# Attention and a gated convolution block on one Trainium2 core: the diagonal masks of the first seven pairs as 64-row blocks, and a start planned with the port shared by DVE and POOL

## The chip, the core and the metric

The kernel runs on one core of one Trainium2 chip. Times are device microseconds of that core; lower is better. The engines are called as in the profile: PE (matrix multiply), DVE (vector), ACT (scalar), POOL (GpSimd) and SP, which here only issues DMAs. Two memories on the core matter: SBUF, and PSUM, into which PE writes. The kernel before took 766.73 us in the median of three runs (767.42, 766.73 and 760.02).

## What is computed

Eight batches of eight heads, 576 positions, head size 64. Each head has its own decay sequence `s`; its prefix sum becomes a bias on the scores. The result of attention goes, per batch, through a block with a three-tap convolution and a sigmoid gate.

```python
scores = scale * np.matmul(q, k.transpose(0, 1, 3, 2))
cum = np.cumsum(np.maximum(s, 0.0), axis=-1)
bias = -(cum[:, :, :, None] - cum[:, :, None, :])
scores = np.where(causal, -1000000000.0, scores + np.minimum(bias, 0.0))
attn = exp(scores - max);  attn = attn / (sum(attn) + 1e-09)
x = attn @ v                      # then, per batch, all heads side by side
h = np.maximum(x @ w_in, 0.0)     # 512 -> 1024
conv_out[t] = sum over k of conv_w[k] * h[t + k - 1]
out = (h * sigmoid(conv_out)) @ w_out
```

## The kernel before, in words

**Work units.** Two heads make a pair; there are 32 pairs, four to a batch. A pair's keys and queries lie in SBUF with head 0 in rows 0 to 63 and head 1 in rows 64 to 127, so that a matmul of one head uses one half of PE's rows. For a pair `p` the steps are:

- load of keys and queries (`raw`, 576 KB, L1015), rounding to the matrix format on ACT or DVE (`hi`, L1027), the remainder on POOL or DVE (`lo`, L1031);
- the row maxima: PE computes the scores (`sh_mm`, L1097), DVE adds the prefix sum of the keys (`bb`, a 576 KB load broadcast from `cum_d`, L1059) and takes the maximum in one instruction (`sh_max`, L1129). 14 such instructions a pair. Six PSUM banks serve all of this, and a bank is free again when the last reader is through;
- PE transposes the maxima (`tn`, L1155), ACT writes them out (`rt`, L1163), a DMA puts them into row 9 of `eq` (`ds`, L1171);
- the scores proper (`sc_mm`, L1208: three matmuls of the split operands and one with `ek`, `eq` that adds the bias), ACT's exponentials (L1223), POOL's causal zeroes (L1241);
- row sums on PE (`sum`, L1323), their reciprocal by way of DRAM: `rc` (L1345), DVE's reciprocal (L1350), `ri` to DRAM (L1355), `rb` back, broadcast (L1365); the product with the values (`pv`, L1266), the scaling (`nm`, L1373) and the split of the result (`xh` L1388, `xl` L1392).

After four pairs a batch goes through the block: L1423 (`h`), L1436 to L1484 (convolution and gate), L1512 (`o`). Its weights are converted from the 64-bit words in which they come (L880 to L956) during the first 110 us.

**Masks in the first seven pairs.** The maximum has to leave out the keys behind the query. From pair 7 on POOL writes -1e30 into the key sums (`cut`, L1070). In pairs 0 to 6 (`early`) PE adds a mask to the scores instead: where a piece ends at the diagonal, a matmul of a 128x128 identity (`unit`) with a triangular `mask` adds -1e30 (L1104). A pair has five such places, four with 128 columns and one with 64, and two heads: 10 mask matmuls a pair, 70 in all. They take all 128 rows of PE, the matmuls around them 64.

**The start.** `s` is loaded (L748); DVE forms the prefix sum (`cum_chain`, L763 and L764), from it `grid` and `ncr` (L771 to L777), then `bx` (L798, L802), which becomes `rows_d` in DRAM. `cum_d` (L789) and `base_d` (L791) are written to DRAM as soon as they exist; `bb` of pair 0 reads `cum_d`.

**What sets the order.** Every step is a task with an engine or a choice of engines, a duration in us and a due time (table `DUE`, in sixteenths of a us). `Sched.play` goes through a model of the engines and takes at each point the task that is due first among those that can start; the order that it finds is written out. An engine then works through its list in order, and so does SP's DMA list. A third field `True` in a DVE or POOL option says that the task uses the port that the two engines share, and the planner then never lets a marked task of one run beside a marked task of the other. Where PE has nothing to do in the plan within its first 112 us (`AWAKE`), a matmul on a zero tile is put in (`stay_awake`, L1559, tile `still`; 241 of them before).

```python
    def play(self, idle=None):
    ...
                    if needs and other and (lock[other] or yields(other, at)):
                        continue
```

## Time and profile before

| | |
|---|---|
| median of three runs | 766.73 us (760.02 to 767.42) |
| profiled execution | 766.71 us, span 765.0 us |
| PE busy | 744.2 us, 97% of the span |
| DVE, ACT, POOL busy | 513.5, 455.6, 363.1 us |
| mean granted clock of PE | 0.989 of full speed |
| `still` matmuls | 241, busy 35.9 us |
| mask matmuls (L1104) | 70, busy 10.3 us |

The span is the time from the first to the last instruction of the profiled execution. The busy time of an engine is the union of its instructions, and matmuls overlap: a single one lasts longer than the distance to the next. Idle time is put down to what ended it. PE's clock is given as a share of full speed: 1.00 is the upper of its two levels (2.4 GHz), 0.50 the lower (1.2 GHz).

### The profile page before, as it was taken

To read this page: it belongs to the slowest core of one execution; us is meant where nothing else is said; L and a number is where in the kernel's file an instruction comes from. 1 tells how busy PE (TensorE), PEld (TensorE's weight loads), DVE (VectorE), ACT (ScalarE), POOL (GpSimd) and SP (SyncE) were. 2 spreads that over 40 slices of the span, in tenths; PEclk is the share of its full clock that TensorE was granted. 3 is DMA by queue.
4 is the path that set the end of the run, shared out by engine and by line. 5 is a ranking of instruction groups with operands and counts; after the bars stand their busy time and mean duration, and the time that the engine had idled before them with its cause. 6 is when DMAs were issued, how large, how long until landed. Compare 5 with 4: busy or idle time off the path is not lost.

```text
span 765.0 us, 20449 instructions
## 1 busy us (share of the span) xinstructions
PE 744.2 (97%) x7868; PEld 669.3 (87%) x7868; DVE 513.5 (67%) x1404; ACT 455.6 (60%) x1070; POOL 363.1 (47%) x444
## 2 busy tenths in 40 slices
PE   8998999999999999999999999999999999999998
PEld 6675778898988888898988889898888999899998
DVE  7488987566776757677775776777686676633632
ACT  5276777375665656566674756556566646654643
POOL 6053435574566455545554655545435546612212
PEclk9599999999999999999999999999999999999999
DMA  6865852324333241424322342242414221111001
GB/s 192 262 212 185 271 185 66 129 66 128 93 106 111 56 128 65 128 93 122 98 79 87 98 132 79 78 143 80 127 48 122 90 82 43 43 41 40 17 25 39
DMA packets 55160, 80.18 MB, mean 105 GB/s; under 512 B 14042, under 2 KB 34842, under 8 KB 55002
## 3 DMA queue, kind: packets, MB, share of 16 engines
q1 hardware_dynamic: 55061, 78.87, 33.3%
q8 instruction: 61, 1.00, 0.5%
q14 instruction: 38, 0.30, 0.1%
HBM read 67.48 MB, written 10.98 MB: 103 GB/s over the span
## 4 chain that ended last, share of the span: by engine, by line
PE 79%; DVE 8%; issue 5%; DMA 4%; ACT 2%; POOL 1%; SPq 0%; DVEq 0%; POOLq 0%; ACTq 0%
PE ps L1423 25%; PE ps L1512 25%; PE ps L1208 11%; PE pv L1266 10%; PE ps L1097 4%; DVE ps L1129 3%; PE ps L1323 3%; DMA rb<-ri_d 2%; DMA ri_d<-ri 2%; ACT pt L1223 1%; PE ps L1559 1%; DVE r L1129 1%; DMA bb<-cum_d 1%; DVE ct L1454 1%; DVE rb L1373 1%
## 5 line engine op out<-in xcount | busy, mean ns | idle before, releaser
L1512 PE MATMUL ps<-u,wo 128*128 128x288 f32 x1536 | 218.2, 298 | 1.1 <-ACT ob L1529 0.5
L1423 PE MATMUL ps<-x,wi 128*128 128x290 f32 x1536 | 217.6, 298 | 0.3 <-DVE x L1392 0.2
L1423 PEld LDWEIGHTS ps<-x,wi 128*128 128x128 f32 x1536 | 209.2, 190 | 2.2 <-ACT pt L1223 0.5
L1512 PEld LDWEIGHTS ps<-u,wo 128*128 128x128 f32 x1536 | 206.9, 188 | 4.0 <-ACT pt L1223 1.7
L1223 ACT ACTIVATE pt<-ps,bias_sb 128x288 f32<-128x288 f32 (+4 forms) x384 | 152.9, 479 | 64.6 <-PE ps L1208 64.4
L1484 POOL TENSOR_TENSOR u<-ct,u 128x576 fp32r<-128x576 f32 x64 | 92.4, 1446 | 187.8 <-ACT u L1480 144.1
L1454 DVE SCALAR_TENSOR_TENSOR ct<-ps,cw_sb,ct 128x288 f32<-128x288 f32 (+1 forms) x256 | 130.2, 514 | 69.6 <-ACT ct L1441 67.1
L1129 DVE CUSTOM_DVE_ANT_0 ps<-ps,bb 128x64 f32<-128x64 f32 (+4 forms) x320 | 134.3, 451 | 47.3 <-PE ps L1097 23.1
L1208 PE MATMUL ps<-s 64*128 64x288 f32 (+4 forms) x1152 | 113.8, 304 | 8.6 <-DVE r L1129 7.5
L1208 PEld LDWEIGHTS ps<-s 64*128 64x128 f32 x1152 | 91.0, 187 | 17.3 <-DVE r L1129 12.4
L1241 POOL TENSOR_SCALAR_AFFINE_SELECT pt<-pt 128x256 f32<-128x256 f32 (+1 forms) x160 | 69.9, 450 | 74.6 <-ACT pt L1223 56.4
L1070 POOL TENSOR_SCALAR_AFFINE_SELECT bb<-bb 128x256 f32<-128x256 f32 (+1 forms) x125 | 52.6, 429 | 98.4 <-DVE r L1129 81.9
L1266 PE MATMUL pv<-pt,v 128*32 128x448 f32 (+4 forms) x1536 | 94.6, 389 | 3.3 <-DVE rb L1373 3.3
L1436 ACT ACTIVATE ps<-ps 128x289 f32<-128x289 f32 x128 | 50.8, 397 | 72.8 <-PE ps L1423 67.1
L1031 POOL TENSOR_TENSOR s<-raw,s 128x1152 fp32r<-128x1152 f32 x31 | 88.8, 2865 | 6.2 <-ACT s L1027 3.9
L1266 PEld LDWEIGHTS pv<-pt,v 128*32 128x32 f32 x1536 | 59.2, 110 | 34.6 <-issue 24.6
L1466 ACT ACTIVATE ct<-ct 128x288 f32<-128x288 f32 x128 | 56.2, 440 | 38.6 <-DVE ct L1454 38.0
L1472 DVE TENSOR_TENSOR ct<-ct,ps 128x288 f32<-128x288 f32 x128 | 57.1, 449 | 21.7 <-ACT ct L1466 20.9
L1441 ACT ACTIVATE ct<-ps,cw_sb 128x288 f32<-128x288 f32 x128 | 63.8, 500 | 5.0
L1097 PE MATMUL ps<-s 64*128 64x288 f32 (+4 forms) x384 | 60.3, 348 | 1.3 <-DVE ct L1472 1.1
L1208 PE MATMUL ps<-eq,ek 64*128 64x288 f32 (+4 forms) x384 | 59.7, 301 | 0.0
L1129 DVE DVE_READ_ACCUMULATOR2_ANT r<- 128x1 f32 x384 | 54.1, 141 | 0.0
(89 smaller groups left out, 700.6 us busy)
## 6 DMA issues: line engine op xcount, KB each, us to landing
raw<-qk SPq DMA_DIRECT2D x32, 576.0 KB
bb<-cum_d SPq DMA_DIRECT2D x32, 576.0 KB
v<-vp SPq DMA_DIRECT2D x32, 320.0 KB
rb<-ri_d SPq DMA_DIRECT2D x64, 144.0 KB
outT<-ob SPq DMA_DIRECT2D x64, 144.0 KB
w<-w_in SPq DMA_DIRECT2D x8, 512.0 KB
w<-w_out SPq DMA_DIRECT2D x8, 512.0 KB
rows_d<-bx SPq DMA_DIRECT2D x1, 1215.0 KB
```

The costliest lines, as they stand in the source:

```text
L1031: tt_on(e)(st[:, 0:2, :], R_t[raw.slot], st[:, 2:4, :].bitcast(F32), op=ALU.subtract)
L1097: nc.tensor.matmul(dst[j], l, S_t[sb.slot][r, 2, c0:c1], start=True, stop=not (early and diagonal(tau, c1)),)
L1129: nc.vector.tensor_tensor_reduce(out=src, in0=src, in1=in1, scale=1.0, scalar=acc if c0 else -3.0e38, op0=ALU.add, op1=ALU.max, accum_out=acc,
L1208: nc.tensor.matmul(dst[j], l, m, start=(k == 0), stop=(k == 3))
L1223: nc.scalar.activation(PT_t[pts[j].slot][0:jt, O_T[t] + c0 : O_T[t] + c1], bank(pb, o, o + c1 - c0)[0:jt], AF.Sigmoid, bias=bias_sb[0:jt, ...
L1241: nc.gpsimd.affine_select(out=reg, in_=reg, pattern=[[0, 2], [1, min(P, W_T[t])]], compare_op=ALU.is_ge, fill=0.0, base=0, channel_multipl ...
L1266: nc.tensor.matmul(pvt[gs, o0 : o0 + c1 - c0], vt[0:jt, t, gs], PT_t[pts[g // 2].slot][0:jt, O_T[t] + c0 : O_T[t] + c1], start=(t == 0), s ...
L1423: nc.tensor.matmul(bank(hb, 0, XW), l, r, start=(k == 0), stop=(k == len(seq) - 1))
L1441: nc.scalar.activation(C_t[ct.slot][:, i, :], bank(hb, 2 * hf, 2 * hf + HS), AF.Copy, scale=cw_sb[:, 3 * f + 1 : 3 * f + 2],)
L1454: nc.vector.scalar_tensor_tensor(cc[:, lo:hi], bank(hb, hf + sh + lo, hf + sh + hi), cw_sb[:, 3 * f + k : 3 * f + k + 1], cc[:, lo:hi], op ...
L1484: tt_on(e)(uu[:, 1], C_t[ct.slot], uu[:, 0].bitcast(F32), op=ALU.subtract)
L1512: nc.tensor.matmul(bank(pb, 0, HS), l, r, start=(fp == 0 and k == 0), stop=(fp == NF // 2 - 1 and k == len(seq) - 1),)
```

## The change

Three things are changed. The mask tile gets 192 columns instead of 384, and each half of its rows holds the same triangle of 64; the mask of a place at the diagonal is now added in blocks of 64 columns, each with a matmul over the 64 rows of PE that belong to the head. A pair has 18 of these instead of 10, 126 in all, each 64 columns wide, and weights and moving operand have changed places (`mask` is loaded, `unit` streams). The planner gets other durations for a handful of tasks, and `cum` and `grid` carry the mark of the shared port. And the table of due times is another one, so that all five lists are in another order.

```diff
 DUE = (
-    -4437, -31564, -3194, -3762, -3297, -3396, -3426, -2970, -2895, -2949, -3684, -32749, -26067,
...
-    MW = 3 * P
+    MW = P + D
...
         nc.gpsimd.memset(mask, 0.0)
-        nc.gpsimd.affine_select(
-            out=mask[:, MW - P : MW], in_=mask[:, MW - P : MW], pattern=[[-1, P]],
-            compare_op=ALU.is_ge, fill=NEG, base=0, channel_multiplier=1,
-        )
-
+        for j in range(2):
+            half = mask[D * j : D * j + D]
+            nc.gpsimd.affine_select(
+                out=half, in_=half, pattern=[[1, MW]], compare_op=ALU.is_ge, fill=NEG,
+                base=-D, channel_multiplier=-1,
+            )
...
-    t_masks = add("masks", [("POOL", 3.6)], [], -190, c_masks)
+    t_masks = add("masks", [("POOL", 4.4)], [], -190, c_masks)
...
-    t_ident = add("ident", [("POOL", 4.3)], [], -189.5, c_ident)
+    t_ident = add("ident", [("POOL", 2.9)], [], -189.5, c_ident)
...
-    t_ones = add("ones", [("DVE", 0.4)], [], -298, lambda e: nc.vector.memset(ones, 1.0))
+    t_ones = add("ones", [("DVE", 0.55)], [], -298, lambda e: nc.vector.memset(ones, 1.0))
...
-    t_cum8 = add("cum", [("DVE", 2.0)], [t_s, t_ones], -170, cum_chain)
+    t_cum8 = add("cum", [("DVE", 2.0, True)], [t_s, t_ones], -170, cum_chain)
...
-    t_cum = add("grid", [("DVE", 2.4)], [t_cum8], -169, grid_chain)
+    t_cum = add("grid", [("DVE", 1.5, True)], [t_cum8], -169, grid_chain)
...
-    t_rest = add("rest", [("DVE", 1.6, True)], [t_cum], -140, rest)
+    t_rest = add("rest", [("DVE", 0.8, True)], [t_cum], -140, rest)
...
-    t_bmm = add("bias_mm", [("PE", 1.2)], [t_rest, t_ident], -140, bias_mm, alloc=[b_ps])
+    t_bmm = add("bias_mm", [("PE", 0.6)], [t_rest, t_ident], -140, bias_mm, alloc=[b_ps])
...
                     if early and diagonal(tau, c1):
-                        dg = min(P, c1)
-                        for j in range(2):
-                            nc.tensor.matmul(
-                                dst[j][:, c1 - dg - c0 : c1 - c0], unit, mask[:, MW - dg : MW],
-                                start=False, stop=True,
-                            )
+                        blocks = (0,) if c1 < P else (D, 0)
+                        for k, at_ in enumerate(blocks):
+                            e0 = c1 - c0 - D * (len(blocks) - k)
+                            for j, r in enumerate(lanes):
+                                nc.tensor.matmul(
+                                    dst[j][:, e0 : e0 + D], mask[r, at_ : at_ + P], unit[r, r],
+                                    start=False, stop=at_ == 0,
+                                )
...
-            t_mm = add(f"sh{p}.{i}", [("PE", SH_D[i] + 0.36 * early * sum(diagonal(tau, c1) for tau, _, c1 in part))],
+            t_mm = add(f"sh{p}.{i}", [("PE", SH_D[i] + 0.23 * early * sum(diagonal(tau, c1) for tau, _, c1 in part))],
```

Three pieces of the new order follow. In the changed file the line numbers are 2 higher from L737 on (L1097 becomes L1099) and 4 higher from L1104 on (L1129 becomes L1133).

First SP's DMA list at the very start, before and then now; `raw` is keys and queries, `pt<-s` the load of the decay sequence, `v` the values, `bb` the broadcast prefix sum of pair 0 (`bb_91`) and pair 1 (`bb_92`).

```order
1 L748 DMA pt<-s 64x576
2 L1015 DMA raw_81<-qk 128x1152
3 L1015 DMA raw_82<-qk 128x1152
4 L880 DMA ht<-cw 128x48
5 L789 DMA cum_d<-pt 64x576
6 L791 DMA base_d<-ncr 64x10
7 L1059 DMA bb_91<-cum_d 128x2x576
8 L1015 DMA raw_81<-qk 128x1152
9 L1059 DMA bb_92<-cum_d 128x2x576
```

```order
1 L1017 DMA raw_81<-qk 128x1152
2 L750 DMA pt<-s 64x576
3 L1017 DMA raw_82<-qk 128x1152
4 L882 DMA ht<-cw 128x48
5 L791 DMA cum_d<-pt 64x576
6 L1017 DMA raw_81<-qk 128x1152
7 L1022 DMA v_94<-vp 128x640
8 L793 DMA base_d<-ncr 64x10
9 L1061 DMA bb_91<-cum_d 128x2x576
10 L1061 DMA bb_92<-cum_d 128x2x576
```

The load of pair 0's keys and queries now stands ahead of the load of `s`, and two bulk loads (`raw` of pair 2 and `v` of pair 0) stand ahead of `base_d` and of the first `bb`.

Second DVE's list over the prefix sum, before and then now; `s_83` and `s_84` are the operands of pairs 0 and 1, whose remainder L1031 (now L1033) forms.

```order
6 L763 TENSOR_SCALAR pt<-pt 64x576
7 L764 SCALAR_TENSOR_TENSOR pt<-pt 64x576
8 L771 TENSOR_SCALAR big<-pt 64x1
9 L772 TENSOR_SCALAR pt<-pt,big 64x576
10 L773 TENSOR_SCALAR pt<-pt,big 64x576
11 L774 TENSOR_SCALAR ncr<-pt 64x9
12 L777 MEMSET ncr 64x1
```

```order
6 L765 TENSOR_SCALAR pt<-pt 64x576
7 L766 SCALAR_TENSOR_TENSOR pt<-pt 64x576
8 L1033 TENSOR_TENSOR s_83<-raw_81,s_83 128x1152
9 L773 TENSOR_SCALAR big<-pt 64x1
10 L774 TENSOR_SCALAR pt<-pt,big 64x576
11 L775 TENSOR_SCALAR pt<-pt,big 64x576
12 L776 TENSOR_SCALAR ncr<-pt 64x9
13 L779 MEMSET ncr 64x1
14 L1033 TENSOR_TENSOR s_84<-raw_82,s_84 128x1152
```

Pair 0's remainder was POOL's and is now DVE's, between the prefix sum and `grid`; POOL has no remainder to form until pair 2, and forms `v_95` (the 0/1 pattern for `eq`) and the pads of `ek` in its place.

Third PE's list in pair 1's maxima, at the two diagonal places of one part (448 and 64 columns), before and then now; `ps` are PSUM banks.

```order
263 L1097 MATMUL ps_68<-s_84 128x448
264 L1097 MATMUL ps_70<-s_84 128x448
265 L1104 LDWEIGHTS unit
266 L1104 MATMUL ps_68<-mask,unit 128x128
267 L1104 LDWEIGHTS unit
268 L1104 MATMUL ps_70<-mask,unit 128x128
269 L1097 MATMUL ps_68<-s_84 128x64
270 L1097 MATMUL ps_70<-s_84 128x64
```

```order
337 L1099 MATMUL ps_65<-s_84 128x448
338 L1099 MATMUL ps_67<-s_84 128x448
339 L1108 LDWEIGHTS mask
340 L1108 MATMUL ps_65<-unit,mask 128x64
341 L1108 LDWEIGHTS mask
342 L1108 MATMUL ps_67<-unit,mask 128x64
343 L1108 LDWEIGHTS mask
344 L1108 MATMUL ps_65<-unit,mask 128x64
345 L1108 LDWEIGHTS mask
346 L1108 MATMUL ps_67<-unit,mask 128x64
347 L1099 MATMUL ps_65<-s_84 128x64
348 L1099 MATMUL ps_67<-s_84 128x64
```

Two mask matmuls of 128 columns have become four of 64. In the rest of PE's list the number of `still` matmuls goes from 241 to 303: ahead of the first matmul of real work 46 instead of 48, between pair 0's first maxima and the transposes of the bias (L830, now L832) 79 instead of 56, from there to the last transpose before the first scores 36 instead of 28 (15 among the maxima instead of 9, 21 instead of 19 behind them), then 2 instead of 5, between pair 0's scores and its sums 30 instead of 16, and in the four rounds after that 110 instead of 88. All other matmuls are the same in number: 1536 of L1423, 1536 of L1512, 1536 of L1208, 384 of L1097.

## Rows read from the trace of the kernel before

**Rows 1.** The busy time of the engines in three stretches of the span (start and end in us, length, then busy us and number of instructions of PE, of its weight loads, of DVE, ACT and POOL, then PE's granted clock, the share of the DMA engines, GB/s).

```profile
18.00:34.50 16.50, 16.49 (x84) 10.18 (x84) 9.19 (x44) 1.92 (x7) 0.00 (x0) 0.50 0.95 294
...
41.73:105.48 63.75, 60.19 (x894) 44.21 (x893) 54.36 (x155) 46.24 (x102) 25.20 (x30) 1.00 0.70 227
105.48:765.00 659.52, 645.08 (x6708) 597.43 (x6702) 432.37 (x1165) 390.32 (x933) 320.15 (x379) 1.00 0.28 86
```

**Rows 2.** The first two of these stretches, only the `still` matmuls (L1559): busy us of PE and of its weight loads, then clock and DMA as above.

```profile
18.00:34.50 16.50, 8.03 (x33) 4.64 (x33) 0.50 0.95 294
...
41.73:105.48 63.75, 12.57 (x89) 7.30 (x88) 1.00 0.70 227
```

**Rows 3.** The chain that ended last, cut to 0 to 42 us (start, us, what).

```profile
7.07 3.22 DVE ncr L774
...
10.86 5.21 DMA bb<-cum_d
...
26.98 4.17 PE ps L1559 x19
...
31.55 1.07 PE ps L1559 x5
32.62 4.54 PE ps L1208 x44
```

**Rows 4.** DVE's instructions in order of time (start, duration, engine, line, operation; in brackets the idle time before and what ended it).

```profile
3.78 0.61 DVE L763 TENSOR_SCALAR pt<-pt 64x576 f32<-64x576 f32 x1
4.42 1.35 DVE L764 TENSOR_TENSOR_SCAN pt<-pt 64x576 f32<-64x576 f32 x1
5.80 0.14 DVE L771 TENSOR_SCALAR big<-pt 64x1 f32<-64x1 f32 x1
...
12.06 1.34 DVE L1031 TENSOR_TENSOR s<-raw,s 128x1152 fp32r<-128x1152 f32 x1
16.25 0.23 DVE L1129 CUSTOM_DVE_ANT_0 ps<-ps,bb 128x64 f32<-128x64 f32 x1 [2.85 <-DMA bb<-cum_d]
...
28.55 0.14 DVE L1129 DVE_READ_ACCUMULATOR2_ANT r<- 128x1 f32 x1
```

**Rows 5.** POOL's instructions in order of time, around the long `ncr` and around DVE's remainder of pair 1.

```profile
7.06 2.64 POOL L1031 TENSOR_TENSOR s<-raw,s 128x1152 fp32r<-128x1152 f32 x1 [1.55 <-ACT s L1027]
...
12.69 1.29 POOL L705 TENSOR_SCALAR_AFFINE_SELECT v<-v 64x640 f32<-64x640 f32 x1
14.05 0.71 POOL L709 TENSOR_SCALAR_AFFINE_SELECT v<-v 64x640 f32<-64x640 f32 x1
```

**Rows 6.** ACT's first two roundings, each started by the landing of a `raw` load.

```profile
5.76 1.15 ACT L1027 CAST s<-raw 128x1152 fp32r<-128x1152 f32 x1 [3.68 <-DMA raw<-qk]
7.76 1.15 ACT L1027 CAST s<-raw 128x1152 fp32r<-128x1152 f32 x1 [0.84 <-DMA raw<-qk]
```

**Rows 7.** PE's instructions in order of time: the `still` matmuls before the transposes of the bias and these transposes, the first sums, the scores of 64 columns and what follows them (the piece of 320), a diagonal place of the maxima with its masks, and two `pv`.

```profile
9.59 6.28 PE L1559 MATMUL pv<-still 64*128 64x256 bf16 x56
17.59 0.70 PE L830 MATMUL ps<-ident,pt 64*128 64x64 f32 x5 [1.71 <-DVE r L1129]
...
41.73 1.77 PE L1323 MATMUL ps<-pt,onehot 128*32 128x144 f32 x54
...
48.49 0.41 PE L1208 MATMUL ps<-s 64*128 64x64 f32 x6
...
48.86 0.74 PE L1208 MATMUL ps<-s 64*128 64x320 f32 x6
...
52.29 0.47 PE L1097 MATMUL ps<-s 64*128 64x448 f32 x2
52.69 0.28 PE L1104 MATMUL ps<-mask,unit 128*128 128x128 bf16 x2
52.91 0.30 PE L1097 MATMUL ps<-s 64*128 64x64 f32 x2
...
58.59 2.90 PE L1266 MATMUL pv<-pt,v 128*32 128x128 f32 x48 [0.99 <-DVE rb L1373]
...
74.13 2.90 PE L1266 MATMUL pv<-pt,v 128*32 128x128 f32 x48 [1.73 <-DVE rb L1373]
```

**Rows 8.** DVE alone from the landing of the first `bb` to the last maximum of pair 1 (length, busy us and number, PE's granted clock, DMA).

```profile
16.20:28.75 12.55, 10.94 (x52) 0.56 0.95 289
```

**Rows 9.** The chain that ended last, cut to 60 to 110 us: the scores of a later pair.

```profile
77.30 3.53 PE ps L1208 x48
```

**Rows 10.** ACT's exponentials of a whole pair at full clock, and the first conversion of a weight piece behind them.

```profile
62.88 4.53 ACT L1223 ACTIVATE pt<-ps,bias_sb 128x288 f32<-128x288 f32 x12
67.27 0.80 ACT L891 ACTIVATE w<-w,tail_sb 128x512 uint32<-128x512 uint8 x1
```

**Rows 11.** SP's issue of the first and of a later `rc`.

```profile
43.92 1.24 SPq L1345 DMA_DIRECT2D rc<-rs x2
...
73.40 1.28 SPq L1345 DMA_DIRECT2D rc<-rs x2
```

**Rows 12.** DVE's reciprocals that read them.

```profile
47.71 0.21 DVE L1350 RECIPROCAL ri<-rc 128x9 f32<-128x9 f32 x1
...
78.39 0.21 DVE L1350 RECIPROCAL ri<-rc 128x9 f32<-128x9 f32 x1
```

**Rows 13.** What PE waited for from 105 us to the end, longest first (engine, line, what ended it: us in total, times, longest).

```profile
PE ps L1208 <- DVE r L1129: 7.5, 19, 0.5
```

468 rows, old and new, of the table DUE are left out of this document.

## The prediction

> **What bounds the kernel now.** I read first the table of stretches. From 105.5 us to the end PE is busy for 645.1 of 659.5 us at full clock [rows 1], it holds no `still` matmul there, and the largest of its waits comes to 7.5 us in 19 pieces [rows 13]: this part is PE's work and nothing else. Before 105.5 us it is another kernel. PE has 12.6 us of `still` matmuls between 41.7 and 105.5 us [rows 2], that is, room; DVE is busy for 54.4 of 63.8 us there. One stretch stands out: from 18.0 to 34.5 us the granted clock is 0.50, the lower level, and 8.0 of PE's 16.5 us are `still` matmuls [rows 1, 2]. So the time is the moment at which PE's dense part begins, plus about 660 us.
>
> Then the chain of waits for the front [rows 3]. Three pieces in it belong to no useful matmul: `ncr`, nine elements wide, that takes DVE 3.22 us; the first `bb`, issued behind it and landing 5.2 us later; and 4.17 us for 19 `still` matmuls behind pair 1's maxima. The list of DVE and that of POOL explain the first: POOL's `lo` runs from 7.06 for 2.64 us on the shared port, and `ncr` is stuck from 7.07 to 10.29 [rows 4, 5]. PE's list explains the last: PE sits idle for 1.71 us before L830 [rows 7], the clock is at its lower level right after, and 19 `still` matmuls that would last 19 x 0.112 = 2.1 us (56 last 6.28 us at full clock [rows 7]) take twice that, while DVE's last maximum, for which the next transpose waits, is done at 28.7 [rows 4].
>
> **The start, moved.** With `raw` ahead of `s` in SP's list, `raw` lands first. The two `raw` land 2.0 us apart [rows 6]; `s` is a quarter of their bytes, 0.5 us. So `raw` lands about 5.25 and `s` about 5.75, where DVE starts on it at 3.78 now [rows 4]: +1.95. Prefix sum, from L763 to L771: 2.02. Then `lo` of pair 0, now DVE's: 1.34. L771 to L774: 7.07 - 5.80 = 1.27. `ncr` without POOL's `lo` beside it: that no row shows; I take 0.2, near L771's 0.14, with 3.22 as the other end. It ends at 5.75 + 2.02 + 1.34 + 1.27 + 0.2 = 10.6 instead of 10.3. The wait at the port is gone and the time is spent elsewhere.
>
> On SP `raw` of pair 2 (waits for `lo`, about 9.1) and `v` are issued before, so `base_d` goes out at 10.7 and `bb` at about 11.2 instead of 10.86. Their 904 KB, at 2.0 us per 576 KB, are 3.1 us of transfer ahead of `bb`; begun at about 10.4, they end at 13.5. I let the first `bb` land 0.7 us later than now; ends +0.3 (only the issue counts) and +1.6 (all of it queues). First maximum: 16.95.
>
> **The clock.** The bias transposes wait for a bank that the third maximum frees. Now 1.34 us lie between the first maximum and L830 (16.25 to 17.59), with columns of 64, 448 and 288; with 448, 448 and 288 it is some 0.4 more: L832 at 16.95 + 1.75 = 18.7. PE's `still` matmuls before it start at 9.59 now [rows 7], and 0.3 to 0.8 earlier with two fewer ahead and cheaper masks; 79 last 8.85 us, so they end near 17.9. The gap is about 0.8 us (0.2 to 1.7) instead of 1.71. A gap of 0.99 us before a later `pv` left the clock at full speed, and so did one of 1.73 [rows 1, 7]: gaps like the one of now go either way, shorter ones show no fall. I take it that the clock holds.
>
> **What that is worth.** DVE needs 10.94 busy us for the maxima of both pairs [rows 8], and PE at full clock doesn't hold it up: 16.95 + 10.94 + 0.3 for small waits = 28.2. Transpose 0.3, two `still` 0.2: scores at 28.7 instead of 32.6, -3.9. They take 3.53 us [rows 9] instead of 4.54: -1.0. Behind them 30 `still` instead of 16: +14 x 0.112 = +1.6. The sums begin at 41.73 [rows 7] - 3.9 - 1.0 + 1.6 = 38.4, less the masks. ACT is no bound: 28.7 + 0.5 + 4.53 + 1.6 for the two conversions of a weight piece that are put between (0.80 for one [rows 10]) ends at 35.3, POOL's last zeroes some 0.6 later.
>
> **The masks.** A place of 128 columns costs PE 0.22 us from the first mask to the next score matmul [rows 7]. Four matmuls of 64 columns: eight such steps of the scores take 0.37 us [rows 7], so 0.18. That is 0.04 a place, 0.2 us a pair. What the change between 128 and 64 rows costs the matmuls around it is not in a row by itself; the two score matmuls of 448 columns before a mask take 0.40, while six of 320 columns in the scores last 0.74 together [rows 7], so it is between 0 and 0.2 a place. I take 0.4 us a pair, and count it once, in pair 2's maxima, which stand between the first scores and the first sums: -0.4. In the other pairs DVE and the DMAs hold the chain, and the plan itself puts 110 `still` where 88 were.
>
> By TensorEngine Tiling (Array Packing), Key Properties, in the Trainium skill, a change of the tiling mode drains TensorE; by it each place is worth the full 0.2, and if PE were the bound the five places of the four rounds would give 4 us. The row with 12.6 us of `still` speaks against PE as the bound.
>
> **The rounds and the rest.** In round 0 the reciprocal runs 47.71 - 45.16 = 2.55 us after the issue of `rc` ends, in round 2 3.71 us after [rows 11, 12], without idle time on DVE: so up to 1.16 us of it are weight pieces ahead in DVE's list. Fewer stand there in the new one in rounds 1 to 3. Ends 0 and -2.3; against it two or three weight loads change places with the small transfers, 0 to +1.5. I take -1.0 together. After 105.5 us the matmuls are the same in number and almost in sequence: 0 +/- 1.5.
>
> **Sum.** -3.9 - 1.0 + 1.6 - 0.4 - 1.0 = -4.7 on the profiled 766.71 us, which is the median to 0.02: **762.0 us**. Bounds of this case: 759.1 to 764.6.
>
> **Rivals.** *The clock falls all the same.* For it: the 1.71 us gap did it, and `bb` behind two bulk loads may land 1.6 us later. Against it: the gap is planned away. Price: L832 1.1 later, six more `still` among the maxima and two more behind at 0.22 each (4.17 / 19) +1.8, three fewer before the scores -0.7, masks -0.7, +1.6 behind the scores and -0.4, -1.0 in the rounds: +1.7, so **768.4** (766 to 770). Slower than before; it decides if the gap stays near the 1.71 us of now.
>
> *The wait at the port only changes its place.* POOL's selects and memsets (0.7 us each) now run beside all of DVE's prefix sum. Two DVE instructions held up for 0.7 us each make `bb` 1.4 us later, the clock falls, and the price is 1.4 more: **769.8**. For it: a select that takes 0.71 took 1.29 beside DVE's `lo` [rows 4, 5]. Against: there POOL waited and DVE's 1.34 us were whole.
>
> By the GPSIMD Engine Reference, Specifications, in the Trainium skill, POOL shares its SBUF interfaces with VectorE and contends with two-port modes and with two SBUF inputs. That fits the 3.22 us, and it speaks against this change, since the scan and `lo` have two inputs; it doesn't say who yields.
>
> *PE's saving reaches the end.* With 0.24 us a place in four rounds, 5 x 4 x 0.24 = 4.8 us less: **757.2**. For it: the chain passes PE's scores and maxima. Against: PE idles before `pv` for DVE [rows 7].
>
> *The order doesn't matter:* the dense part begins where it did, 766.7. This lies between the first two cases.
>
> **How the numbers follow.** Forecast 0.57, clock falls 0.20, port 0.08, PE's saving 0.15. The range leaves out the lowest and highest tenth: 757.0 to 769.5. One per cent of the median is 7.7 us, about what can be told here. Faster than 759.1: most of PE's saving and a sixth of the forecast case, 0.22. Slower than 774.4 takes the port case with a second loss as large: 0.04. Within: 0.74.
>
> **What would show it.** `ncr` under 0.4 us; `s` landing after the first `raw`; first `bb` between 16.4 and 17.7; the gap before L832 near 0.8 us; the granted clock at 1.00 from 18 to 34 us; scores of pair 0 before 30 us, sums before 39; the first L1427 near 101. I am wrong if the clock is at 0.50 there, if `bb` lands after 18, or if the dense part takes over 661.5 us.

## The result, and the profile after

The changed kernel takes 774.89 us in the median of four runs (772.22 to 778.40), the kernel before 764.0 (four runs): ratio 1.0133, 95% interval 1.0084 to 1.0182. It is slower by 1.3%; predicted were 762.0 us, 757.0 to 769.5.

For each run PE's mean granted clock is known, and the time goes with it: over 109 runs taken beside the experiments the kernel before takes 761.1 us (median of 26) at a mean clock of 0.998 or more and 767.1 (median of 72) at 0.991 or less. Its profiled run of 766.71 is one of the latter. The profiled run of the changed kernel (772.22, mean clock 0.987) is the fastest of its four.

The stretches of the changed kernel: 18 to 34.5 us as in [rows 1], then from the first sums to the first L1427, then the dense part (columns as there).

```profile
18.00:34.50 16.50, 14.33 (x99) 10.71 (x101) 10.48 (x50) 1.20 (x5) 0.00 (x0) 0.60 0.94 307
42.40:109.00 66.60, 62.26 (x947) 47.13 (x946) 54.95 (x153) 48.06 (x104) 27.55 (x33) 0.95 0.74 225
109.00:770.50 661.50, 648.69 (x6709) 598.79 (x6702) 416.86 (x1154) 392.90 (x933) 330.68 (x388) 1.00 0.28 85
```

Against [rows 1] the 5.5 us between the two spans fall into four pieces: first sums 41.73 to 42.40 (+0.7), from there to the fifth sums 58.2 to 61.4 (+3.2), on to the dense part 5.6 to 5.2 (-0.4), dense part 659.5 to 661.5 (+2.0). The first sums and the rounds were forecast to come out 3.7 and 1.0 us shorter.

DVE over the prefix sum and at the first maximum, to be read against [rows 4], and three of POOL's selects beside it.

```profile
5.25 0.91 DVE L765 TENSOR_SCALAR pt<-pt 64x576 f32<-64x576 f32 x1 [1.39 <-DMA pt<-s]
6.19 1.75 DVE L766 TENSOR_TENSOR_SCAN pt<-pt 64x576 f32<-64x576 f32 x1
7.87 1.86 DVE L1033 TENSOR_TENSOR s<-raw,s 128x1152 fp32r<-128x1152 f32 x1
...
9.83 0.93 DVE L774 TENSOR_SCALAR pt<-pt,big 64x576 f32<-64x576 f32 x1
10.79 0.84 DVE L775 TENSOR_SCALAR pt<-pt,big 64x576 f32<-64x576 f32 x1
11.67 0.51 DVE L776 TENSOR_SCALAR ncr<-pt 64x9 f32<-64x9 f32 x1
...
18.42 0.63 DVE L1133 CUSTOM_DVE_ANT_0 ps<-ps,bb 128x448 f32<-128x448 f32 x1 [3.05 <-DMA bb<-cum_d]
```

```profile
5.12 0.72 POOL L710 TENSOR_SCALAR_AFFINE_SELECT v<-v 64x640 f32<-64x640 f32 x1
5.89 0.84 POOL L706 TENSOR_SCALAR_AFFINE_SELECT v<-v 64x640 f32<-64x640 f32 x1
6.80 1.72 POOL L710 TENSOR_SCALAR_AFFINE_SELECT v<-v 64x640 f32<-64x640 f32 x1
```

Nearly every DVE step of the chain lasts longer than in [rows 4]: the scan 1.75 for 1.35, `lo` 1.86 for 1.34. One of POOL's selects pays too, 1.72 for 0.72. The first maximum comes 2.2 us later than 16.25. PE's list shows what hangs on it, and a second loss.

```profile
20.17 0.51 PE L832 MATMUL ps<-ident,pt 64*128 64x64 f32 x5 [2.69 <-DVE r L1133]
...
57.44 3.33 PE L1327 MATMUL ps<-pt,onehot 128*32 128x144 f32 x56
```

The idle time before the bias transposes is 2.69 us instead of 1.71 [rows 7], and the clock is at 0.50 from about 21.3 to 35 us (13.2 of these 16.5 us, by the mean of 0.60). At 57.44 the sums of pair 1, 1.8 us at full clock, take 3.33: a second fall, from about 55.4 to 62.2 us, which the profile before doesn't have.

### The profile page after: what moved, and what is told of

Same layout as the page of the kernel before. It is cut to its first block, busy times and chain, and to the rows that moved or that the text cites. A ratio compares the mean times of both kernels' runs of the same rounds, so it can differ in the third digit from the quotient of the medians.

```text
span 770.5 us, 20687 instructions
## 1 busy us (share of the span) xinstructions
PE 749.3 (97%) x7986; PEld 676.7 (88%) x7986; DVE 499.6 (65%) x1392; ACT 460.2 (60%) x1072; POOL 373.9 (49%) x455
## 4 chain that ended last, share of the span: by engine, by line
PE 82%; DVE 6%; DMA 5%; ACT 3%; issue 3%; SPq 0%; POOL 0%; DVEq 0%; ACTq 0%; POOLq 0%
PE ps L1516 26%; PE ps L1427 25%; PE pv L1270 11%; PE ps L1212 11%; PE ps L1099 4%; PE ps L1327 4%; DVE ps L1133 3%; DMA bb<-cum_d 1%; ACT pt L1227 1%; DMA rb<-ri_d 1%; PE ps L1563 1%; DMA ri_d<-ri 1%; DVE r L1133 1%; DMA w<-w_out 1%; DVE ct L1458 1%
## 5 line engine op out<-in xcount | busy, mean ns | idle before, releaser
L1427 PE MATMUL ps<-x,wi 128*128 128x290 f32 x1536 | 219.2, 298 | 1.7 <-DVE ct L1476 1.6
L1427 PEld LDWEIGHTS ps<-x,wi 128*128 128x128 f32 x1536 | 209.6, 190 | 3.8 <-DVE ct L1476 2.2
L1227 ACT ACTIVATE pt<-ps,bias_sb 128x288 f32<-128x288 f32 (+4 forms) x384 | 154.6, 478 | 65.1 <-PE ps L1212 64.5
L1458 DVE SCALAR_TENSOR_TENSOR ct<-ps,cw_sb,ct 128x287 f32<-128x287 f32 (+1 forms) x256 | 129.8, 514 | 72.6 <-ACT ct L1445 70.1
L1133 DVE CUSTOM_DVE_ANT_0 ps<-ps,bb 128x448 f32<-128x448 f32 (+4 forms) x320 | 134.0, 453 | 56.7 <-PE ps L1099 30.9
L1212 PE MATMUL ps<-s 64*128 64x288 f32 (+4 forms) x1152 | 117.3, 305 | 6.0 <-DVE r L1133 5.4
L1212 PEld LDWEIGHTS ps<-s 64*128 64x128 f32 x1152 | 94.0, 187 | 16.0 <-DVE r L1133 11.8
L1245 POOL TENSOR_SCALAR_AFFINE_SELECT pt<-pt 128x256 f32<-128x256 f32 (+1 forms) x160 | 66.4, 427 | 76.5 <-ACT pt L1227 46.9
L1033 POOL TENSOR_TENSOR s<-raw,s 128x1152 fp32r<-128x1152 f32 x30 | 84.6, 2821 | 6.3 <-DVE s L1029 4.3
L1212 PE MATMUL ps<-eq,ek 64*128 64x288 f32 (+4 forms) x384 | 62.2, 300 | 0.0
L1099 PE MATMUL ps<-s 64*128 64x288 f32 (+4 forms) x384 | 59.5, 348 | 1.5 <-DVE ct L1476 0.6
L1133 DVE DVE_READ_ACCUMULATOR2_ANT r<- 128x1 f32 x384 | 54.5, 142 | 0.0
```

What stands on the lines that cost most here:

```text
L1033: tt_on(e)(st[:, 0:2, :], R_t[raw.slot], st[:, 2:4, :].bitcast(F32), op=ALU.subtract)
L1099: nc.tensor.matmul(dst[j], l, S_t[sb.slot][r, 2, c0:c1], start=True, stop=not (early and diagonal(tau, c1)),)
L1133: nc.vector.tensor_tensor_reduce(out=src, in0=src, in1=in1, scale=1.0, scalar=acc if c0 else -3.0e38, op0=ALU.add, op1=ALU.max, accum_out=acc,
L1212: nc.tensor.matmul(dst[j], l, m, start=(k == 0), stop=(k == 3))
L1227: nc.scalar.activation(PT_t[pts[j].slot][0:jt, O_T[t] + c0 : O_T[t] + c1], bank(pb, o, o + c1 - c0)[0:jt], AF.Sigmoid, bias=bias_sb[0:jt, ...
L1245: nc.gpsimd.affine_select(out=reg, in_=reg, pattern=[[0, 2], [1, min(P, W_T[t])]], compare_op=ALU.is_ge, fill=0.0, base=0, channel_multipl ...
```

## The experiments

All medians stand beside the kernel before on the same chip (11 to 33 runs in each of five sets: 766.0, 761.7, 766.3, 766.5, 767.1 us). `move` takes tasks out of the list that `play` returned and puts them in elsewhere; everything else stays in its order. The letters are the theories named in the expectations.

| run | median us (range) | ratio to before, 95% interval |
|---|---|---|
| e1 still before L832 | 773.3 (769.8 to 776.4) | 1.0086 (1.0052 to 1.0120) |
| e2 new order, old masks | 778.2 (777.2 to 781.2) | 1.0158 (1.0128 to 1.0189) |
| e3 old order, new masks | 766.1 (761.7 to 774.1) | 1.0010 (0.9977 to 1.0042) |
| e4 before, still before L830 | 765.1 (760.8 to 769.5) | 0.9987 (0.9955 to 1.0018) |
| e5 round 2 moved | 775.4 (772.4 to 776.8) | 1.0155 (1.0117 to 1.0192) |
| e6 s first | 774.7 (773.1 to 776.4) | 1.0145 (1.0109 to 1.0182) |
| e7 POOL late | 775.5 (773.6 to 780.0) | 1.0165 (1.0124 to 1.0207) |
| e8 old dense order | 773.4 (772.4 to 774.9) | 1.0134 (1.0094 to 1.0173) |
| e9 weights moved | 778.8 (778.0 to 780.6) | 1.0191 (1.0155 to 1.0227) |
| e10 three at once | 776.7 (773.5 to 777.4) | 1.0146 (1.0111 to 1.0182) |
| e11 before, weight late | 769.6 (763.8 to 773.5) | 1.0034 (1.0004 to 1.0064) |
| e12 before, still on all rows | 762.0 (760.7 to 765.6) | 0.9976 (0.9949 to 1.0003) |
| e13 changed, still on all rows | 773.0 (769.0 to 775.5) | 1.0088 (1.0060 to 1.0116) |
| e14 e3 and e12 | 764.7 (762.3 to 769.9) | 0.9999 (0.9969 to 1.0029) |
| e15 changed, six weights out | 769.1 (766.6 to 771.0) | 1.0040 (1.0016 to 1.0064) |
| e16 before, six weights out | 766.2 (760.2 to 768.1) | 0.9997 (0.9966 to 1.0028) |
| e17 e4 and e12 | 762.8 (760.2 to 764.6) | 0.9956 (0.9933 to 0.9979) |
| e18 e13 and e6 | 771.9 (770.2 to 775.4) | 1.0079 (1.0051 to 1.0107) |

**The start: DVE and POOL on one port.** e7 holds POOL back until `ncr` exists.

```diff
+    move(["masks", "pads2", "pads1"], after="grid")
+    move(["ind2", "ind1", "ind0"], after="bx3")
+    move(["v0"], after="ind0")
...
         for t in order:
+            if t is t_masks:
+                nc.gpsimd.tensor_copy(ind[0:64, 0:1], ncr[0:64, 1:2])
             t.emit(t.eng)
```

> The changed kernel with POOL's column masks (L703 to L710) and its two `ek` memset groups behind DVE's `ncr`: a one-column copy of ncr on POOL holds them back, and ACT's three copies of the masks and the load of pair 0's values go behind the `bx` steps. So POOL does nothing on the shared port while DVE runs the prefix sum, lo and grid. Theory I (the port stretches DVE): scan 1.35 us (1.75 in the changed kernel), lo 1.34 (1.86), the two grid steps 0.51 each (0.93, 0.84), ncr under 0.2 (0.51): ncr ends at 10.0 to 10.3 instead of 12.2, first maximum at 16.3 to 16.7 instead of 18.4, and 1 to 2 us less in all, 773 to 774. Rival J (DVE is slower there for another reason, such as the loads that land in SBUF meanwhile): the durations stay, ncr at 12.

DVE in e7:

```profile
6.03 0.45 DVE L765 TENSOR_SCALAR pt<-pt 64x576 f32<-64x576 f32 x1 [2.17 <-DMA pt<-s]
6.51 1.35 DVE L766 TENSOR_TENSOR_SCAN pt<-pt 64x576 f32<-64x576 f32 x1
7.79 1.32 DVE L1033 TENSOR_TENSOR s<-raw,s 128x1152 fp32r<-128x1152 f32 x1
...
9.21 0.51 DVE L774 TENSOR_SCALAR pt<-pt,big 64x576 f32<-64x576 f32 x1
9.76 0.51 DVE L775 TENSOR_SCALAR pt<-pt,big 64x576 f32<-64x576 f32 x1
10.31 0.16 DVE L776 TENSOR_SCALAR ncr<-pt 64x9 f32<-64x9 f32 x1
```

These are the durations of theory I, to 0.02 us. Loads went on landing meanwhile, so J is out. The first maximum came at 17.38, 1.0 earlier (`s` itself landed 0.8 later in this run). The end did not move: 775.5, against 773 to 774 expected.

The Trainium skill, Trainium Architecture — The Big Picture (What this means for kernel authors), says that engines and DMAs can't contend in SBUF, and that DVE and GpSimd contend for a port pair that is an exclusive lock, not a bandwidth split. The first agrees with e7. The second fits the rows as well: `ncr` waited for all of `lo` [rows 3, 5]. In the changed kernel the scan began at 6.19, with 0.54 us left of a select, and took 0.40 longer; the next select, at 6.80, had the scan before it until 7.94 and took 1.00 longer; `lo`, at 7.87, had 0.65 us of that select before it and took 0.52 longer. POOL's times are rough, so this is a reading and not a proof; no run separates a lock from a split.

e6 undoes one move of SP's list and puts the load of `s` ahead of `raw` again: `move(["s"], before="qk0")`.

> The changed kernel with the load of `s` ahead of `raw` again, as in the kernel before; all else is the order of the change. s lands at about 3.7 instead of 5.25 us, raw 0.5 later. Theory H (bb is late by the sum of s's 1.5 us and of the stretched DVE steps): ncr ends 1.0 to 1.5 earlier, first maximum at 17.0 to 17.4 instead of 18.4, 1 to 1.5 us less in all, 773 to 774. Rival I (POOL's selects and memsets set the pace of DVE whenever they run): DVE's steps are stretched more, because POOL's list begins no later, ncr at 11.5 or later, first maximum within 0.5 of 18.4, total unchanged.

`ncr` ended at 10.5 and the first maximum came at 16.54, so H held there. The first sums came at 39.70, 2.7 us earlier, and the end where it was, at 774.7:

```profile
39.70:112.61 72.91, 63.79 (x948) 47.48 (x947) 55.85 (x160) 47.73 (x102) 28.20 (x33) 0.93 0.69 200
```

From first sums to dense part 72.9 us instead of 66.6, at a mean clock of 0.93. e18 repeats it where the clock mostly holds.

> The changed kernel with `still` matmuls on all rows and the load of `s` ahead of `raw`. If the start's lateness reaches the end, the first maximum comes 1.5 to 2 us earlier and the time falls from 773.0 to about 771 (767 to 768 in runs at full clock, where the edit with the rows alone gave 769.0 to 770.0). If the rounds swallow it, the first sums come earlier and the time stays at 772 to 774 (769 to 770 at full clock).

Median 1.1 us under e13; in runs at 0.998 or more 770.2, 770.4 and 771.6 against e13's 769.0 to 772.9. The first maximum came only 0.4 earlier than in e13's profile (17.21, 17.58), so it tests little. By both, an earlier start brought 0 to 1 us in the new order; that the clock alone ate more in e6 isn't excluded. Other pairs of profiles pass an earlier start on whole: in the old order from the profile before to e17's (first sums 41.73 and 36.04, dense part from 105.48 and 99.41), in the new one from the changed kernel's to e13's (42.40 and 39.38, 109.00 and 105.80), where the clock held throughout in e13 and e17, which follow below.

**The clock.** e1 and e4 fill the idle time before the bias transposes, e1 with 24 `still` matmuls, e4 with 16.

```diff
         for t in order:
+            if t is t_bmm:
+                for _ in range(24):
+                    stay_awake(-1, None, 0)
             t.emit(t.eng)
```

> The changed kernel with 24 more `still` matmuls on PE right before the bias transposes (L832), written into the bank of `pv`, which is not in use yet. 24 x 0.112 = 2.7 us fill the 2.69 us for which PE idles there. Nothing else is changed. Theory A (the late bb opens the gap, the gap lets the clock fall, and the fall is what the start loses): the granted clock stays 1.00 from 18 to 34.5 us, DVE then paces both pairs' maxima: first maximum 18.4 + 10.9 + 0.3 = 29.7, scores of pair 0 near 30.2 instead of 32.9, 1 us shorter, sums near 39.8 instead of 42.4 (1.6 of it given back by `still` matmuls behind the scores if more of them fit); total 2 to 4 us under the changed kernel, 771 to 773. Rival B (the clock falls for what PE does, not for this gap): clock 0.50 again somewhere from 18 to 34.5, total within 1 us of the changed kernel, 774 to 776. Rival C (the time is lost in the rounds and the dense part, the start does not count): clock holds, scores early, but the dense part begins at 109 as before: 774 to 776.

> The kernel before with 16 more `still` matmuls (16 x 0.112 = 1.8 us) before the bias transposes (L830), written into the idle bank of `pv`. It prices the clock's fall with no other change. Theory A: clock 1.00 from 18 to 34.5 us, scores of pair 0 at 16.25 + 10.94 + 0.3 + 0.5 = 28.0 instead of 32.6 and 1 us shorter; with 1.6 us given back behind the scores 3 to 5 us less in every run: 759 to 761, and the spread of the runs (760 to 767) goes to its lower end. Rival B: the clock falls all the same, 764 to 767. Rival C (the rounds hold the end): clock holds, time within 1 us of the kernel before.

e4's stretch from 18 to 34.5 us, and its L830:

```profile
18.00:34.50 16.50, 16.25 (x93) 10.48 (x92) 8.85 (x41) 2.54 (x8) 0.23 (x1) 0.63 0.88 264
```

```profile
18.21 0.51 PE L830 MATMUL ps<-ident,pt 64*128 64x64 f32 x5
```

No idle time is left before L830, PE is busy for 16.25 of 16.50 us, and the clock fell all the same, at about 22 us instead of 17.8 (means of 0.63 and 0.50). Theory A falls: the gap alone is not what lets it fall, though the fall came later without it. In e1 the low stretch shrank to 3.3 us (mean 0.90), a second one as long came from about 54 to 57 us, the first sums came at 40.3, the dense part at 108.3 instead of 109.0, and 770 to 776 us were left: nearest to rival C.

e12 changes what PE does there: with `r = slice(0, P)` in `stay_awake` all `still` matmuls use 128 rows.

> The kernel before with every `still` matmul on all 128 rows of PE instead of 64 where its neighbours use 64; their number and places stay. In the runs of the kernel before the mean granted clock goes with the time: 0.998 to 1.000 with 760.6 to 763.0 us, 0.989 with 765.8 to 769.1. Theory O (the stretch with `still` matmuls of 64 rows and small real work is where the clock is lost, and it can be kept by what PE does there): mean clock 0.996 or more in most runs, 761 to 763. Rival P: the same spread of clocks as the kernel before, or 1 to 2 us more because the `still` matmuls now differ from their neighbours in the rows they use.

The mean clock was 0.998 or more in 9 of 12 runs (6 of 23 of the kernel before on this chip), the median 762.0 beside 766.3, as theory O had it. e17 adds e4's sixteen.

> The kernel before with every `still` matmul on all 128 rows and 16 more of them before the bias transposes (L830). With the rows alone the clock stayed at 0.998 or more in 9 of 12 runs (762.0). If the 1.7 us of idle time before L830 are what lets it fall in the others, it stays at 0.998 or more in nearly all runs here, 761 to 762 with a spread under 3 us. If the idle time doesn't matter, the same mixture of clocks as with the rows alone.

The mean clock was 0.999 or more in 11 of 12 runs (2 of 19 before, at 0.998 or more), and this is the only version whose interval lies under the kernel before:

```profile
18.00:34.50 16.50, 15.79 (x148) 11.39 (x146) 10.26 (x44) 6.13 (x17) 3.29 (x4) 1.00 0.94 290
```

9 of 12 and 11 of 12 are too close to say whether the idle time counts beside the rows. Nor do the rows hold the clock by themselves: e14 and e16 below have them too, on another chip and with a second edit each, and were at 0.998 or more in 0 and 3 of 12 runs (6 of 33 before); their profiles show 0.69 and 0.59 from 18 to 34.5 us. e13 gives the changed kernel the same rows.

> The changed kernel with every `still` matmul on all 128 rows of PE. If the order is what costs (start, rounds, dense part) and the clock only adds to it, the clock goes to 0.995 or more in most runs and the time to 769 to 771: 8 us above the kernel before with the same edit (762.0), 4 to 5 us under the changed kernel. If the changed kernel loses by the clock alone, it comes to 762 to 764.

The median, 773.0, lies above both ranges. The three runs at a mean clock of 1.000 take 769.0 to 770.0, 8 to 9 us above the median of the kernel before at 0.998 or more: that is lost without the clock. Here is e13 from the first sums to the dense part, then e17:

```profile
39.38:105.80 66.42, 60.80 (x947) 45.75 (x947) 54.74 (x155) 47.40 (x102) 27.14 (x32) 1.00 0.73 225
```

```profile
36.04:99.41 63.37, 61.06 (x893) 44.02 (x893) 54.65 (x155) 47.46 (x104) 25.24 (x30) 1.00 0.72 228
```

**The masks.** e2 and e3 exchange them, in either order; e14 is e3 with the clock of e12.

```diff
-                        dg = min(P, c1)
...
+                        blocks = (0,) if c1 < P else (D, 0)
```

> The changed kernel's order with the old masks: one 128-row matmul per head and place (70 in all instead of 126), mask tile 384 columns wide with one select instead of two. Theory D (the 64-row blocks cost the time: they leave PE's array half unused and PE quicker through, so that the clock falls a second time near 56 us): no second fall, dense part begins 2 to 3 us earlier, 771 to 773. Rival E (the order costs it): the second fall stays or the masks' own 0.2 us a pair are added: 775 to 777. POOL has one select less before DVE's prefix sum: both theories allow the first maximum up to 0.7 us earlier.

> The kernel before, its table of due times and its planned durations, with only the mask tile and the mask matmuls of the change. Theory D (the 64-row blocks cost the time): a second fall of the clock in the rounds and 767 to 771. Rival E (the order costs it, the blocks save what they are shorter by): no second fall, 762 to 764, that is 0 to 2 us under the kernel before (0.4 in the start, the rest covered by DVE).

> The kernel before with the 64-row mask blocks of the change and every `still` matmul on all 128 rows. If the blocks shorten the path (0.2 us in each of five maxima, as the prediction had it for one of them), 760 to 761.5 with the clock at 0.995 or more. If DVE and the transfers cover them, 761.5 to 762.5 as without them. If blocks of half the rows cost clock, 764 to 767 with the clock under 0.993.

e3 shows no difference that can be told (766.1 lies between the two ranges) and no second fall in its profile, and e2 has falls without the blocks; D falls. e14 took 764.7 at clocks of 0.989 to 0.996, lower than e12's and nearest to the third outcome. So no gain from the blocks can be seen, and whether they cost clock is open. e2's profile has three falls, and its runs are slower than the changed kernel's median, but the intervals overlap.

**The dense part.** e8 takes the due times of the kernel before for tasks planned after 95 us.

> The changed kernel with the due times of the kernel before for all tasks that its plan starts after 95 us; the plan up to the dense part is the changed one, row for row. Theory K (the new order of the dense part costs by itself): from the first L1427 on 659.5 to 660.0 us as in both profiles with the old table (659.5, 659.6, 660.1), instead of 661.1 to 661.6 as in the three with the new one, so 1 to 2 us less in all, 773 to 774. Rival L (the dense part is longer for what the front leaves behind, late transfers and conversions): 661 or more again.

```profile
110.44:770.60 660.16, 645.43 (x6708) 597.54 (x6702) 432.67 (x1163) 389.54 (x931) 322.91 (x381) 1.00 0.28 86
```

The dense part takes 660.2 us, 1.3 less than 661.5, as theory K had it; the median is 1.5 less too, but the runs of the two kernels overlap (772.4 to 774.9, 772.2 to 778.4). Over all profiles, e9 and e10 apart, it is 659.5 to 660.2 us in the old order and 661.1 to 661.7 in the new one.

**The rounds.** A round's chain runs from the reciprocal (L1350, L1354) by `ri` and `rb` to DVE's scaling (L1373, L1377), which frees the bank for the next `pv`. SP's list in round 2, before and then after:

```profile
75.48 0.39 SPq L1059 DMA_DIRECT2D bb<-cum_d  x1
75.92 0.46 SPq L880 DMA_DIRECT2D w<-w_in  x1
77.10 0.35 SPq L1020 DMA_DIRECT2D v<-vp  x1
...
78.63 0.34 SPq L1355 DMA_DIRECT2D ri_d<-ri  x1
79.03 0.42 SPq L880 DMA_DIRECT2D w<-w_in  x1
79.50 0.50 SPq L880 DMA_DIRECT2D w<-w_out  x1
...
82.24 1.22 SPq L1365 DMA_DIRECT2D rb<-ri_d  x2
```

```profile
78.00 0.39 SPq L1061 DMA_DIRECT2D bb<-cum_d  x1
79.61 0.34 SPq L1022 DMA_DIRECT2D v<-vp  x1
80.13 0.32 SPq L1359 DMA_DIRECT2D ri_d<-ri  x1
...
81.12 0.88 SPq L882 DMA_DIRECT2D w<-w_out  x2
82.10 0.38 SPq L882 DMA_DIRECT2D w<-w_in  x1
...
84.23 1.20 SPq L1369 DMA_DIRECT2D rb<-ri_d  x2
```

Three weight pieces of 512 KB stand between `ri` and `rb` instead of two, none ahead of `ri` instead of one. DVE's scaling ends the chain, before (its reciprocal is in [rows 12]) and after:

```profile
87.06 0.75 DVE L1373 TENSOR_TENSOR rb<-pv,rb 128x576 f32<-128x576 f32 x1
```

```profile
79.64 0.20 DVE L1354 RECIPROCAL ri<-rc 128x9 f32<-128x9 f32 x1
...
91.97 0.75 DVE L1377 TENSOR_TENSOR rb<-pv,rb 128x576 f32<-128x576 f32 x1
```

This takes 8.7 us before and 12.3 after. The chain that ended last shows, in the changed kernel, what the scaling waited for in this round: not `rb`, but a weight piece and the conversions of it that stand ahead in DVE's list.

```profile
81.12 5.18 DMA w<-w_out
...
88.50 0.59 ACT w L888
...
91.36 0.20 DVE w L897
...
91.97 0.75 DVE rb L1377
```

Over four rounds, reciprocal to scaling takes 38.9 us before and 44.9 after, scaling to the next reciprocal 20.6 and 17.5. Profiles of either order repeat it: 37.5 to 40.7 and 20.4 to 20.7 (e3, e4, e12, e14, e17) against 44.9 to 49.4 and 17.2 to 17.8 (e1, e6, e7, e8, e13, e18).

e11 puts the fault into the kernel before.

```diff
+    move(["wi7"], after="wo1")
+    move(["wi7q", "wi7t"], after="wo1t")
+    move(["wi71"], before="wi72")
```

> The kernel before with the fault put in: in round 2 the load of one weight piece goes from ahead of `ri` to between `ri` and `rb`, as the third there, and its conversions behind those of the other two on ACT, ahead of DVE's L1373 as they were. Theory F2: from reciprocal to L1373 in round 2 grows from 8.7 to 9.7 us (three profiles of the old order) to 12 or more, the reciprocal itself comes up to 1 us earlier, and the end is 1.5 to 3 us later than the kernel before run beside it. Rival N: within 0.7 us of it.

Round 2 takes 11.5 us (72.69 to 84.22), not quite the 12 of F2; the end comes 3.3 us later in the median, and the four runs at 0.998 or more take 763.8 to 764.8 against 760.2 to 763.0. One piece in the wrong place costs about 3 us (0.3 to 4.9 by the interval).

Taking it out of the changed kernel is another matter. e5: `move(["wi7"], after="rb2")` and `move(["nm2"], before="wo21")`.

> The changed kernel with two steps of round 2 moved in the written order: the load of the third weight piece between `ri` and `rb` (512 KB) goes behind `rb`, and DVE's `rb<-pv,rb` (L1377) goes ahead of the weight conversions L897 and L903 instead of behind them. In the profiles of the changed kernel the stretch from reciprocal to L1377 in that round is 12.3 us long (79.64 to 91.97) where it was 8.7 us before (78.39 to 87.06). Theory F (the rounds lose in the transfer of rb behind the weights, and behind their conversions): 512 KB at about 300 KB per us are 1.7 us, and the conversions in front another 1 to 1.3: L1377 at 9 to 9.5 us behind its reciprocal, and 2 to 3 us less in all if the next round keeps it: 772 to 773 against 774.9. Rival G (the loads only change places, the next round waits for the piece instead): the stretch is shorter in round 2, longer in round 3, total within 1 us of the changed kernel.

Round 2 takes 9.5 us, as F had it, but from there to the next reciprocal it is 7.7 instead of 3.2 us, and the chain that ended last now runs through the late piece's load (86.74, 6.0 us) to that reciprocal. Rival G holds. e9 hands all four last pieces on by one place, e10 adds `s` and the dense order.

> The changed kernel with the weight pieces where the kernel before has them: two instead of three loads between `ri` and `rb` of round 2, one piece each handed on to the next place in round 3, and the last one behind the reciprocal of round 4, all with their conversions on ACT, DVE and POOL and their buffers. Nothing else is moved. Theory F2 (the third piece of round 2 costs twice: its 512 KB ahead of rb, and its conversions ahead of DVE's L1377, ACT's sums and the next reciprocal; moving the load alone left the conversions in the way): from reciprocal to L1377 in round 2 about 9.5 us (12.3 in the changed kernel), the next reciprocal no later than 5 us behind L1377, the rounds from the first sums to the fifth about 58.5 to 59.5 us instead of 61.4, and 2 to 3 us less in all: 772 to 773. Rival N (the rounds are held by the clock or by PE, the pieces are only what waits with them): the stretch gets shorter, the rounds stay at 61 or more, 774.5 to 775.5.

> Three of the undone parts at once: `s` ahead of `raw`, the old due times for the dense part, and the weight pieces as in the run with the moved weights. What stays of the change is its masks, its order in the start behind `s` and in the rounds. If the three losses are separate places (start 1.9 us at the first maximum, rounds 3.2, dense part 1.5 to 2.0) they add: first sums at 39.7 to 40.5, dense part from 101 to 104, 660 us long: 763 to 768. If the losses of the rounds are one bottleneck that swallows what the start gains, as with `s` ahead of `raw` alone, it ends at 771 to 773.

Neither helped, and neither theory had e9's 778.8: round 2 stayed at 12.0 and 12.8 us, and the dense part became 664.8 and 664.4 us long, with weight conversions, by the order those of the piece put last, still on its chain at 125 us. These two tell little beyond that.

e15 and e16 leave six weight pieces out of either order, those of its rounds 2 and 3: `order.remove(by[n + x])` for all their tasks, and zeros in their place.

> The changed kernel with `still` matmuls on all rows and without the six weight pieces of rounds 2 and 3 (wo1, wo2, wi7, wo4, wo6, wo7): neither loaded nor converted, zeroed once by POOL in the start, so that these parts of the weights are left out of the result. If the pieces' place among the small transfers is what makes the new rounds longer, rounds 2 and 3 take the same from reciprocal to L1377 in both orders, within 0.7 us, and the stretch from the first sums to the dense part is the same within 1.5 us as in the kernel before with six pieces left out. If the rest of the order costs it, 3 us or more stay between the two.

> The kernel before with `still` matmuls on all rows and without the six weight pieces of its rounds 2 and 3 (wi7, wi6, wo1, wo2, wo4, wo6), zeroed once by POOL in the start: these parts of the weights are left out of the result. From the first sums to the dense part 62.8 to 65.6 us in the profiles of the old order with them; without them 58 to 61. It is the other half of the comparison with the changed kernel without six pieces.

First sums to dense part, e16 and then e15:

```profile
42.77:105.14 62.37, 61.03 (x894) 43.97 (x893) 46.67 (x144) 36.54 (x86) 23.23 (x29) 1.00 0.60 182
```

```profile
41.36:105.73 64.37, 60.41 (x947) 46.16 (x946) 47.32 (x149) 38.47 (x88) 24.41 (x30) 1.00 0.59 183
```

They are 2.0 us apart, between the two bounds set ahead; round 2 takes 8.0 (e16) and 9.8 us (e15), not within 0.7, and e16's 62.4 us miss the 58 to 61 expected. By this the pair is inconclusive. Where the loss lies depends on what one reads it by. By PE's sums it lies in the first two rounds: from first to third sums 27.9 (e16) and 30.9 (e15), from third to fifth 29.6 and 29.1, and the first stretch is 30.0 to 33.7 us in every profile of the new order and 27.5 to 29.3 in every one of the old.

But the sums are not the end of the chain, and by the reciprocals that loss is made up. Here is the first one of the changed kernel, then the third of e17, e13, e16 and e15 (those of the kernel before are in [rows 12]):

```profile
48.67 0.21 DVE L1354 RECIPROCAL ri<-rc 128x9 f32<-128x9 f32 x1
```

```profile
72.61 0.21 DVE L1350 RECIPROCAL ri<-rc 128x9 f32<-128x9 f32 x1
```

```profile
75.69 0.20 DVE L1354 RECIPROCAL ri<-rc 128x9 f32<-128x9 f32 x1
```

```profile
78.50 0.20 DVE L1350 RECIPROCAL ri<-rc 128x9 f32<-128x9 f32 x1
```

```profile
77.95 0.20 DVE L1354 RECIPROCAL ri<-rc 128x9 f32<-128x9 f32 x1
```

From the first to the third reciprocal it is 30.7 us before and 31.0 after, 30.5 in e17 and 30.2 in e13. From the third to the dense part it is 27.1 before and 29.4 after, and at full clock 26.8 (e17) and 30.1 (e13); without the six pieces 26.6 (e16) and 27.8 (e15); with the fault put in 29.9 (e11). Over all profiles it is 26.6 to 29.0 in the old order without the fault and 29.4 to 35.8 in the new one with the pieces. So the loss lies behind the third reciprocal, and by these profiles, one each, the pieces of rounds 2 and 3 make up about two thirds of the 3.3 us at full clock. The rest is open.

## Why the prediction was wrong, step by step

- **`s` at 5.75:** DVE started on it at 5.25. Right in order, 0.5 too late.
- **The DVE chain, 4.8 us with `ncr` at 0.2:** wrong, and the first step to fail. It took 6.9 (5.25 to 12.2), because the durations were those of [rows 4], where POOL did not hold these steps up. With POOL held back (e7) they are the ones forecast. The rival "the wait at the port only changes its place", given 0.08, is what happened: the chain took 2.1 us longer than forecast, in six steps of 0.3 to 0.5 and not in two of 0.7, and with `s` 0.5 earlier the first maximum came at 18.42, 1.5 behind the 16.95, where the rival had 1.4. Its 769.8 was still short by the rounds and the dense part.
- **`bb` +0.7 for the two bulk loads:** about right. From issue to landing it took 5.5 us instead of 5.2 [rows 3], +0.3, where the step had 0.3 for the later issue and 0.4 for the loads. (The loads are 896 KB, not 904.) The rest of the 2.2 us is the later end of `ncr`, 12.2 instead of 10.3.
- **Gap 0.8, so the clock holds:** wrong. The gap was 2.69 and the clock was at 0.50 for 13 us; and e4, where it fell with no gap, shows that the rule behind the step was wrong too.
- **An early start is worth 3.3 us (-3.9, -1.0, +1.6):** not tested as it stands, since the start was late and the clock fell. In e13, where the clock held, the first sums came at 39.4 behind a first maximum at 17.58 (forecast: 38.4 less the masks, behind 16.95), and the dense part 3.2 us earlier than in the changed kernel. In e6 2.7 us at the first sums were lost again by the dense part, at a mean clock of 0.93.
- **Masks -0.4:** e3 puts them at 0 within 0.4%, 3 us, which is too coarse to judge 0.4 us.
- **Rounds -1.0:** wrong in sign, +2.8 with the way to the dense part. Its gain was there, and larger: 3.1 us less from scaling to reciprocal. The term against it, "0 to +1.5" for loads that change places, was mis-sized: +6.0 from reciprocal to scaling, 3.7 of it in round 2, where the scaling stood behind a weight piece's conversions. The term counted loads ahead of the small transfers and left out the conversions ahead of the scaling. Not all of the 6.0 are these pieces: without the six it is 42.9 (e15) against 36.9 (e16).
- **Dense part 0 +/- 1.5:** +2.0, just past it, by the order (e8: 660.2 instead of 661.5).

In the profiled runs the forecast misses by 10.2 us: 4.4 up to the first sums (the DVE chain and the clock), 3.8 from there to the dense part (the rounds) and 2.0 in the dense part. The median lies another 2.7 above the profiled run.

At full clock on both sides, e13's profile against e17's, the sum reads: first sums 39.4 and 36.0 (+3.3), to the dense part 66.4 and 63.4 (+3.1), dense part 661.5 and 659.6 (+1.9), together 8.3 us. Up to 2.8 us of the first term is luck: `ncr` was quick in e17 (below).

## What to carry to other kernels

Take a duration for a moved step from a row that has the same neighbour on the shared port; the row of a quiet moment is a lower bound. Before counting what a step gains by standing earlier, ask what now stands ahead of the next link of the chain: here a weight piece's conversions, ahead of the scaling in DVE's list, made that stretch of round 2 3.7 us longer. When the order is new everywhere, even "the same matmuls" needs a term of its own.

## What the runs showed that was not expected

The long `ncr` [rows 3] is a race. In e11 and e17, with the same order of DVE and POOL there, POOL's `lo` began 0.13 us or more after `ncr`, and `ncr` took 0.17 us; the first maximum came at 13.4 instead of 16.25. POOL and then DVE in e17:

```profile
7.20 3.21 POOL L1031 TENSOR_TENSOR s<-raw,s 128x1152 fp32r<-128x1152 f32 x1 [1.70 <-ACT s L1027]
```

```profile
7.07 0.17 DVE L774 TENSOR_SCALAR ncr<-pt 64x9 f32<-64x9 f32 x1
```

In [rows 3, 5] they began 0.01 us apart, POOL first; in e3, e4, e12 and e16 POOL was 0.02 to 0.16 us ahead, and `ncr` took 2.6 to 3.2 us. And in 18 to 34.5 us PE was busy for 16.49 of 16.50 us in the kernel before, with the clock at 0.50 throughout [rows 1]: a busy PE is no sign of the upper level.
